# A two-layer convolution/MLP training step: layer-1 pre-activations reloaded half a stage ahead, normalised inputs loaded behind them, and w1-gradient transposes put half a job further on

## The chip, the cores and the metric

The kernel runs on one core of a Trainium2 chip. The metric is the device time of one execution in microseconds. A core has five engines that run their own in-order instruction streams: TensorE (PE in the profile, with its weight loads as PEld), VectorE (DVE), ScalarE (ACT), GpSimd (POOL) and SyncE (SP). SP, POOL and ACT also issue the transfers (DMAs) between the chip's main memory and the on-chip memory.

## The reference

The reference computes a forward pass and all its gradients. With `S = 2048` rows, `D = 448` columns and `F = 1792` hidden columns:

```python
def block_A(x):   # q = layernorm(x); k, v, shift_k, ssm_k, ssm_D are inputs
    kv = shift_conv(k, shift_k) * v              # 4 taps along the sequence
    y  = causal_conv(kv, ssm_k) + kv * ssm_D     # over the whole sequence, by FFT
    return layernorm(x) * y

def block_B(x):
    return silu(layernorm(x) @ w1) @ w2          # 448 -> 1792 -> 448

x = A_q
x = x + block_A(x); x = x + block_B(x)           # "layer 0"
x = x + block_A(x); x = x + block_B(x)           # "layer 1"
out, vjp = jax.vjp(whole, A_q, A_k, A_v, A_shift_k, A_ssm_k, A_ssm_D, w1, w2)
return out, *vjp(grad_out)
```

All inputs and outputs are bf16. `y` depends on no layer's `x`, so it is computed once. The weights are shared by the two layers, so their gradients are sums over the two.

## The kernel before, in words

The program has three parts. The prefix computes `y` by matrix FFTs. The main part does the forward pass of both layers and the backward pass through the MLPs. The suffix computes the gradients of the convolution and of the weights.

In the main part the 2048 rows are cut into four chunks `c` of 512 rows. A stage of the backward pass of layer `L` for chunk `c` is `ga(c, L)` followed by `gn(c, L)`:

- `ga` multiplies the incoming gradient (transposed, `gT`) by `w2T` in seven steps `fp`, each of eight matmuls into `ps_g`. ACT copies each result to `ghp` (line 625; one buffer), and DVE multiplies it by the slope of silu, `dT`, into `ghT` (line 630). After steps 3 and 6 half of `ghT` is turned by DMA transposes and stored to `GH_d` (`store_turned`). These go through SP.
- `gn` multiplies `ghT` by `w1T` for each of four 128-row tiles `tl` into `ps_n` (14 matmuls each). ACT scales the result to `lb_u` (line 668), and a chain of some eleven DVE instructions goes back through the two layernorms (`lb_junk`, `lb_cc`, `G`, `gy`, `gYb`), in layer 0 with one more ACT instruction, `lb_v` (line 646).

For layer 1 the slopes are made from pre-activations that are still on the chip. For layer 0 the forward pass stored the pre-activations to the main memory (`DT_d`, two halves per chunk), because they don't fit; `load_d(c, half)` reads a half back (896 KB, tile `dTl`, three buffers under the tag `D`), and `slope` turns it into silu's derivative in place, with four ACT instructions (line 560). `load_n(c)` reads the normalised inputs `nb_l` and `na_l` (448 KB each).

Which instruction comes first on an engine is decided by a scheduler, from the program's order, the readiness of operands and its own estimates; within an engine or a queue the resulting order is fixed. `tc.issue_after(i)` keeps what stands inside it behind instruction `i` in that order. Before the change, in a stage of layer 0, `slope` of the second half is kept behind the last `lb_u` of the stage before (`k.last_u`), and `slope` of the next chunk's first half stands in the middle of `ga`; that half is loaded at the start of the same stage.

The weight gradients in the suffix are jobs (`_job`): a 512 KB tile `dstat` of stored activations (`A_d`) or gradients (`GH_d`) is loaded through SP, and 16 matmuls multiply it by a 1792 KB operand that stays on the chip: `X` and `GO` (the output's gradient) for w2, `mov3` and `mov1` (normalised inputs) for w1. Two jobs add into one `ps_d`, giving 128 of the 1792 rows of a gradient. The first w2 jobs are fillers: they may be scheduled into gaps of TensorE from a given load on. For w1 the 128 x 448 result has to be stored turned: DVE casts it to `dout`, TensorE transposes it in four pieces into `ps_dt`, ACT copies it to `do`, and POOL stores it:

```python
        o = pool.tile([P, D], BF16, name="dout", tag="dout", bufs=2)
        nc.vector.tensor_copy(o[:], ps[:, :D])
        pt = psum.tile([DC, ND, P], BF16, name="ps_dt", tag="po", bufs=2)
        for dc in range(ND):
            nc.tensor.transpose(pt[:, dc, :], o[:, dc * DC:(dc + 1) * DC], k.ident[:])
```

In the built order these four transposes stand 4 matmuls into the next job pair in most cases, and 5 to 10 in the first four. Beside these jobs DVE computes the gradient of `k` (`gkp`, `gk_acc`, `gk`; lines 982 and 984). `GO` takes the place of `w1` (tag `WA`) and `mov3` that of `w2` (tag `WB`), so neither can be loaded before the forward pass of layer 1 has done with these weights. `mov1` takes the place of `X`.

Of the kernel before, what the change touches and what calls it, by code (L numbers as in the profile page):

```python
# [10 lines left out]
FP32 = mybir.dt.float32  # L11
BF16 = mybir.dt.bfloat16
# [5 lines left out]
P = 128  # L18
S = 2048
D = 448  # L20
F = 1792
J = 16
NT = 16
DC = 112
ND = 4
NF = 14
# [222 lines left out]
def _pm(ap2d):  # L249
    return ap2d.rearrange("(p j) d -> p j d", j=J)  # L250
# [213 lines left out]
class Main:  # L464
# [191 lines left out]
    def gn(self, c, L, ghT, nb, gres, na):  # L656
        nc, k = self.nc, self.k
        sl = slice(4 * c, 4 * c + 4)
        si = 2 * L
        cp = self.ch.tile([P, 8, 2], FP32, name="cp", tag="cp", bufs=1)  # L660
        G = k.X[:, sl, :] if L == 1 else self.ch.tile([P, 4, D], BF16, name="G0", tag="gb", bufs=2)
        for tl in range(4):
            t = 4 * c + tl
            pn = k.psum.tile([P, 512], FP32, name="ps_n", tag="tr" if L == 1 and tl % 2 else "po", bufs=2)
            for ft in range(NF):
                nc.tensor.matmul(pn[:, :D], lhsT=ghT[ft // 7][:, ft % 7, tl * P:(tl + 1) * P], rhs=self.w1T[:, ft, :], start=(ft == 0), stop=(ft == NF - 1))  # L666
            u0 = self.ch.tile([P, D], FP32, name="lb_u0", tag="lb_u0", bufs=2)
            last_u = nc.scalar.activation(u0[:], pn[:, :D], ACT.Identity, scale=k.rstd[2 * L + 1][:, t:t + 1], accum_out=cp[:, tl, 0:1])  # L668
            k.bal.add("act", 0.75)
            k.last_u = last_u  # L670
            g1 = G[:, tl, :]
            self.ln_bwd(u0[:], nb[:, tl, :], cp[:, tl, :], gres(tl), g1)
            if L == 1:
                nc.vector.tensor_tensor(out=k.gYb[:, t, :], in0=g1, in1=na[:, tl, :], op=ALU.mult)
            else:
                gy = self.ch.tile([P, D], BF16, name="gy", tag="lb_junk", bufs=1)
                nc.vector.tensor_tensor(out=gy[:], in0=g1, in1=na[:, tl, :], op=ALU.mult)
                nc.vector.tensor_tensor(out=k.gYb[:, t, :], in0=gy[:], in1=k.gYb[:, t, :], op=ALU.add)
            u1 = self.ch.tile([P, D], BF16, name="lb_u1", tag="lb_u0", bufs=2)
            nc.vector.scalar_tensor_tensor(out=u1[:], in0=g1, scalar=k.rstd[si][:, t:t + 1], in1=self.Y[:, t, :], op0=ALU.mult, op1=ALU.mult, accum_out=cp[:, 4 + tl, 0:1])  # L680
            k.bal.add("dve", 1.2)
            self.ln_bwd(u1[:], na[:, tl, :], cp[:, 4 + tl, :], g1, g1, g1 if L == 0 else None)
        if L == 0:
            nc.gpsimd.dma_start(out=_pm(k.outs[1][0])[:, sl, :], in_=G[:])

    def load_d(self, c, hh):
        nc, k = self.nc, self.k
        t = self.td.tile([P, NF // 2, 512], BF16, name="dTl", tag="D", bufs=3)
        k.d0_load = nc.sync.dma_start(out=t[:], in_=k.DT_d[c, hh])
        return t  # L690

    def load_n(self, c):
# [13 lines left out]
    def run(self):  # L706
        k, nc = self.k, self.nc
        pairs = ((0, 2), (2, 4))
        with self.tc.high_priority():
            self.a_fwd(0, 0, k.x0c0, k.na0, pairs)  # L710
            nT = self.b_tr(self.b_pre(0, 1, pairs, nc.vector))
        cur = []
        self.h(0, 0, nT, 0, cur)
        for c in range(4):
            if c < 3:
                self.a_fwd(c + 1, 0, self.x0_load(c + 1))
                nb = self.b_pre(c + 1, 1)
            else:
                na, nb = self.a_fwd(0, 2, None), self.b_pre(0, 3)
            self.h(c, 0, nT, 1, cur)  # L720
            nT = self.b_tr(nb)
            if c in (1, 2):
                self.load_weights_T(3 - c)
            fol = []
            self.h((c + 1) % 4, 0 if c < 3 else 1, nT, 0, fol)
            self.out(c, cur, False)
            cur = fol
        for c in range(4):
            gb, gT = self.g_pre(c, 1)
            self.h(c, 1, nT, 1, cur)  # L730
            if c < 3:
                na1 = self.a_fwd(c + 1, 2, None)
            self.out(c, cur, True)
            self.turn_plain(c)
            if c == 3:
                d0 = self.load_d(0, 0)
                self.slope(d0)
            box = []
            ghT = self.ga(c, 1, gT, cur, (lambda: box.append(self.b_pre(c + 1, 3))) if c < 3 else None)
            cur = []  # L740
            if c < 3:
                nb1 = box[0]
                nT = self.b_tr(nb1)
                self.h(c + 1, 1, nT, 0, cur)
            else:
                d1 = self.load_d(0, 1)
                nl = self.load_n(0)
                gn = self.g_pre(0, 0)
            self.gn(c, 1, ghT, nb, lambda tl: gb[:, tl, :], na)
            na, nb = na1, nb1  # L750
        for c in range(4):
            with self.tc.issue_after(k.last_u.ins):
                self.slope(d1)
            dT, (nb, na), (gb, gT) = ((None, d0), (None, d1)), nl, gn
            if c == 2:
                k.mov3 = k.wk.tile([P, NT, D], BF16, name="mov3", tag="WB")
                with self.tc.issue_after(k.d0_load.ins):
                    nc.sync.dma_start(out=k.mov3[:], in_=_pm(k.N_d[3][:]))
            if c == 1:
                k.GO = k.wk.tile([P, NT, D], BF16, name="GO", tag="WA")  # L760
                with self.tc.issue_after(k.d0_load.ins):
                    nc.sync.dma_start(out=k.GO[:], in_=_pm(k.grad_out[0]))
            if c < 3:
                d0 = self.load_d(c + 1, 0)
            ghT = self.ga(c, 0, gT, dT, (lambda: self.slope(d0)) if c < 3 else None)
            if c < 3:
                d1 = self.load_d(c + 1, 1)
                nl = self.load_n(c + 1)
                gn = self.g_pre(c + 1, 0)
            self.gn(c, 0, ghT, nb, lambda tl: self.X[:, 4 * c + tl, :], na)  # L770
        self.flush()


def _job(k, ps, src, ft, mov, slot, start, stop):
    pl, tag, bufs = slot
    st = pl.tile([P, NT, P], BF16, name="dstat", tag=tag, bufs=bufs)
    k.nc.sync.dma_start(out=st[:], in_=src[:, ft, :, :])
    for t in range(NT):
        i = k.nc.tensor.matmul(ps[:, :D], lhsT=st[:, t, :], rhs=mov[:, t, :], start=start and t == 0, stop=stop and t == NT - 1)  # L779
    return i  # L780
# [15 lines left out]
def _gw1(k, pool, slots, mov3, mov1):  # L796
    nc, psum = k.nc, k.psum
    out7v = k.outs[7].rearrange("(c p) f -> p c f", p=DC)
    for ft in range(NF):
        ps = psum.tile([P, 512], FP32, name="ps_d", tag="tr", bufs=2)  # L800
        for L, mov in ((1, mov3), (0, mov1)):
            slot = slots.pop(0)
            slots.append(slot)
            _job(k, ps, k.GH_d[L], ft, mov, slot, L == 1, L == 0)
        o = pool.tile([P, D], BF16, name="dout", tag="dout", bufs=2)
        nc.vector.tensor_copy(o[:], ps[:, :D])  # L806
        pt = psum.tile([DC, ND, P], BF16, name="ps_dt", tag="po", bufs=2)
        for dc in range(ND):
            nc.tensor.transpose(pt[:, dc, :], o[:, dc * DC:(dc + 1) * DC], k.ident[:])  # L809
        o7 = pool.tile([DC, ND, P], BF16, name="do7", tag="do7", bufs=2)  # L810
        nc.scalar.copy(o7[:], pt[:])  # L811
        nc.gpsimd.dma_start(out=out7v[:, :, ft * P:(ft + 1) * P], in_=o7[:])  # L812


def _ssm_suffix(k):
    nc, tc, bal = k.nc, k.tc, k.bal
# [3 lines left out]
    psum = k.psum  # L820
    mm = dict(tag="mm", bufs=2)
    k.pt = dict(s1=mm, s2=mm, v=mm)
    with ExitStack() as es:
# [7 lines left out]
        dp2 = pool("dp2")  # L831
        A1 = sp.tile([P, NDH, 2, 16, 4], BF16, name="A1g")
        Z = sp.tile([P, NDH, P], BF16, name="Zg")
        ksf = k.yk.tile([P, J, D], BF16, name="ksf", tag="Y")
        B1k = A1[:].rearrange("p a c n s -> p (a c n s)").rearrange("p (q d) -> p q d", d=D)
        _load_minv(k, nc.gpsimd)
# [2 lines left out]
        with tc.tile_pool(name="sspec2", bufs=1, reuse_waits="tile") as p1:  # L839
# [8 lines left out]
            def spectrum(cp):  # L848
# [3 lines left out]
                t = [kk[:, 0, :], kk[:, 1, :], xsw]  # L852
                nc.gpsimd.dma_start(out=t[0], in_=k.SPEC_d["K"][:, lo:hi])
                nc.gpsimd.dma_start(out=t[1], in_=k.SPEC_d["KV"][:, lo:hi])
                if cp == 2:
                    nc.gpsimd.dma_start(out=ksf[:], in_=_pm(k.KS_d[:]))
                for u in range(2):
# [105 lines left out]
            nc.gpsimd.dma_start(out=o4[0:1536].rearrange("(g b n) -> b g n", g=3, b=4), in_=gsk[:, 0:3, :])  # L963
            nc.gpsimd.dma_start(out=o4[1536:1792].rearrange("(b n) -> b n", b=2), in_=gsk[0:2, 3, :])
        slots = [(k.dp, "dstat", 3)]
        with tc.issue_after(k.d0_load.ins):
            _gw2(k, k.dp, range(4), slots)
        slots = [(k.dp, "dstat", 3), (k.dp, "dstat", 3), (dp2, "dstat", 2), (k.dp, "dstat", 3), (dp2, "dstat", 2)]
        _gw2(k, k.dp, range(4, NF), slots)
# [49 lines left out]
```

## Time and profile before

| what | us |
|---|---|
| median of six runs | 798.3 |
| lowest and highest | 796.33 and 800.05 |
| the profiled execution's own time | 796.33 |
| its span from the first to the last instruction | 794.5 |
| PE busy | 724.7 |
| DVE busy | 516.1 |
| ACT busy | 441.0 |
| POOL busy | 101.7 |

The profile is one execution. Its times are counted from the span's start. Engine rows give the start, the duration, the engine, the line, the operation, the tiles written and read, and in square brackets how long the engine stood idle before and what ended that. A `q` behind an engine's name marks its queue of transfers. The mean granted clock of TensorE was 0.972. In this execution the layer-0 stages of the backward pass lie between about 408 and 551 us, and the w1-gradient jobs from 691 us to the end.

### The profile page before, as it was taken

The page shows a single profiled execution, that of the slowest core. Times are in us where ns is not written, and L with a number is a line of the kernel's source. Part 1 is how long each engine was busy: PE and PEld are TensorE (multiplying, and loading weights), DVE is VectorE, ACT ScalarE, POOL GpSimd, SP SyncE. Part 2 cuts the span into 40 slices and gives each one's busy share as a digit, 9 for nine tenths or more (in the row PEclk, how much of TensorE's full clock was granted, in tenths as well). Part 3 has the DMA queues.
Part 4 walks back from the last instruction along what each step waited for, and adds up shares of the span by engine and source line. Part 5 has one row for each costly group of instructions (what it writes and reads, how often), then busy time and mean ns, then how long its engine had stood idle before and what let it go on. Part 6 is the DMA issues. An engine that isn't in the chain of part 4 may idle for free.

```text
span 794.5 us, 12699 instructions
## 1 busy us (share of the span) xinstructions
PE 724.7 (91%) x4982; PEld 380.5 (48%) x5025; DVE 516.1 (65%) x1056; ACT 441.0 (56%) x551; POOL 101.7 (13%) x168
## 2 busy tenths in 40 slices
PE   6998779999999999999979696999799999989995
PEld 4966534444444434434434332444466765545553
DVE  4789678788435978859467875878456625894100
ACT  4879777766466676876846757545356633000000
POOL 1143212222100010000000000001011123111111
PEclk9999889999999999999999998999999999999999
DMA  9359999998968869889878998989978685777650
GB/s 321 130 171 306 374 219 295 296 278 213 259 169 170 176 183 231 205 176 228 212 226 195 277 295 212 285 209 309 365 211 284 200 307 185 257 237 209 177 177 17
DMA packets 188888, 183.69 MB, mean 231 GB/s; under 512 B 135482, under 2 KB 164030, under 8 KB 187804
## 3 DMA queue, kind: packets, MB, share of 16 engines
q1 hardware_dynamic: 173808, 122.77, 59.3%
q0 software_dynamic: 12688, 52.08, 18.9%
q10 hardware_dynamic: 2332, 8.03, 3.3%
q8 instruction: 39, 0.64, 0.3%
q14 instruction: 21, 0.17, 0.1%
HBM read 76.50 MB, written 65.87 MB: 179 GB/s over the span
## 4 chain that ended last, share of the span: by engine, by line
issue 43%; PE 26%; DVE 14%; ACT 8%; POOL 4%; DMA 3%; POOLq 0%; SPq 0%; ACTq 0%; DVEq 0%
PE ps_o L598 6%; PE ps_d L779 5%; PE ps_h L518 5%; DVE dT L113 3%; DMA kk_c<-spec_KV 2%; PE ps_v L232 2%; DVE ln_st L260 2%; PE ps_v L233 2%; ACT na L274 2%; POOL out_dram L812 1%; PE ps_cv L370 1%; PE ps_gK L911 1%; ACT aT L574 1%; POOL rstd L267 1%; ACT ghp L625 1%
## 5 line engine op out<-in xcount | busy, mean ns | idle before, releaser
L779 PEld LDWEIGHTS <-dstat 128*128 128x128 bf16 x896 | 87.1, 99 | 81.6 <-issue 7.7
L518 PE MATMUL ps_g<-gT,w2T 128*128 128x512 bf16 (+1 forms) x432 | 101.7, 396 | 23.0 <-ACT ghp L625 21.4
L518 PE MATMUL ps_h<-nT,w1sb 128*128 128x512 bf16 (+1 forms) x434 | 102.6, 385 | 6.1 <-DVE dT L113 2.6
L666 PE MATMUL ps_n<-w1T,ghT 128*128 128x448 bf16 x448 | 92.4, 353 | 1.9 <-ACT lb_u L668 1.4
L598 PE MATMUL ps_o<-w2sb,aT 128*128 128x448 bf16 x448 | 90.8, 353 | 0.3 <-ACT aT L574 0.3
L779 PE MATMUL ps_d<-mov,dstat 128*128 128x448 bf16 x448 | 88.9, 357 | 0.6 <-DMA mov<-N_d 0.6
L574 ACT ACTIVATE aT<-ps_h 128x1024 bf16<-128x1024 f32 (+1 forms) x64 | 58.3, 918 | 37.5 <-PE ps_h L518 28.7
L518 PEld LDWEIGHTS <-w2T 128*128 128x128 bf16 (+1 forms) x448 | 37.3, 99 | 85.6 <-issue 56.7
L113 DVE CAST dT<-ps_h 128x1024 bf16<-128x1024 f32 (+1 forms) x56 | 59.3, 1066 | 26.0 <-ACT aT L574 25.9
L625 ACT CAST ghp<-ps_g 128x1024 bf16<-128x1024 f32 x56 | 56.5, 1008 | 34.3 <-DVE ghT L630 18.8
L518 PEld LDWEIGHTS <-w1sb 128*128 128x128 bf16 (+1 forms) x448 | 36.3, 97 | 68.3 <-issue 40.4
L666 PEld LDWEIGHTS <-ghT 128*128 128x128 bf16 x448 | 41.7, 98 | 45.3 <-DVE ghT L630 5.1
L598 PEld LDWEIGHTS <-aT 128*128 128x128 bf16 x448 | 42.1, 98 | 43.0 <-issue 4.3
L811 ACT COPY do<-ps_dt 112x512 bf16<-112x512 bf16 x14 | 8.2, 586 | 87.6 <-PE ps_dt L809 87.6
L232 PE MATMUL ps_v<-Gsb,pa 128*128 128x128 bf16 x336 | 42.7, 221 | 10.2 <-DVE Zg L113 5.0
L779 PE MATMUL ps_d<-X,dstat 128*128 128x448 bf16 x224 | 51.5, 364 | 0.2
L779 PE MATMUL ps_d<-GO,dstat 128*128 128x448 bf16 x224 | 50.5, 356 | 0.2
L806 DVE CAST dout<-ps_d 128x448 bf16<-128x448 f32 x14 | 8.7, 624 | 57.3 <-PE ps_d L779 57.3
L233 PE MATMUL ps_v<-Gsb,pb 128*128 128x128 bf16 x336 | 41.7, 221 | 1.0 <-DVE pb L443 0.7
L668 ACT ACTIVATE lb_u<-ps_n,rstd 128x448 f32<-128x448 f32 x32 | 20.3, 634 | 37.0 <-DVE G L653 16.1
L232 PEld LDWEIGHTS <-pa 128*128 128x128 bf16 x336 | 33.2, 99 | 12.1 <-DVE pa L442 7.0
L630 DVE TENSOR_TENSOR ghT<-dT,ghp 128x1024 bf16<-128x1024 bf16 (+1 forms) x32 | 19.5, 620 | 27.6 <-ACT ghp L625 27.6
(187 smaller groups left out, 1180.9 us busy)
## 6 DMA issues: line engine op xcount, KB each, us to landing
GH_d<-turned SPq DMA_DIRECT2D x16, 896.0 KB, 5.8
dstat<-A_d SPq DMA_DIRECT2D x28, 512.0 KB, 5.1
dstat<-GH_d SPq DMA_DIRECT2D x28, 512.0 KB, 3.8
A_d<-turned SPq DMA_DIRECT2D x12, 896.0 KB, 4.8
DT_d<-dT POOLq DMA_DIRECT2D x8, 896.0 KB, 6.3
dTl<-DT_d SPq DMA_DIRECT2D x8, 896.0 KB, 6.7
spec_K<-Z POOLq DMA_DIRECT2D x7, 512.0 KB, 7.9
KB<-Z POOLq DMA_DIRECT2D x14, 256.0 KB, 12.0
```

The lines of the kernel that those rows point to most:

```text
L113: eng.tensor_copy(out, in_)
L232: nc.tensor.matmul(pv[:, i, :], lhsT=pa[:, i * P:(i + 1) * P], rhs=k.Gsb[:, ga, :], start=True, stop=False)
L233: nc.tensor.matmul(pv[:, i, :], lhsT=pb[:, i * P:(i + 1) * P], rhs=k.Gsb[:, gb, :], start=False, stop=True)
L260: i = nc.vector.bn_stats(out=st[:, tl, :], in_=src(tl))
L518: self.nc.tensor.matmul(ps[:, u, :], lhsT=w[lo:hi, b, f:f + P], rhs=x[lo:hi, b, :], start=(seen[u] == 1), stop=(seen[u] == ND))
L574: last = nc.scalar.activation(a, ps[:, 0:n, :], ACT.Silu)
L598: nc.tensor.matmul(po[:, :D], lhsT=aT[ft // 7][0][:, ft % 7, tl * P:(tl + 1) * P], rhs=self.w2sb[:, ft, :], start=(ft == 0), stop=(ft == N ...
L625: k.last_gh = nc.scalar.copy(gh[:], ps[:])
L630: nc.vector.tensor_tensor(out=ghT[hh][:, o:o + len(u), :], in0=dT[hh][1][:, o:o + len(u), :], in1=gh[:, u[0]:u[0] + len(u), :], op=ALU.mult)
L666: nc.tensor.matmul(pn[:, :D], lhsT=ghT[ft // 7][:, ft % 7, tl * P:(tl + 1) * P], rhs=self.w1T[:, ft, :], start=(ft == 0), stop=(ft == NF - 1))
L668: last_u = nc.scalar.activation(u0[:], pn[:, :D], ACT.Identity, scale=k.rstd[2 * L + 1][:, t:t + 1], accum_out=cp[:, tl, 0:1])
L779: i = k.nc.tensor.matmul(ps[:, :D], lhsT=st[:, t, :], rhs=mov[:, t, :], start=start and t == 0, stop=stop and t == NT - 1)
```

## The change

In layer 0 of the backward pass the first half of the next chunk but one is now loaded behind the second half of the next chunk, at the end of `ga`, so that there are always up to three halves on the chip (`e0` is the third). `slope` of the second half is kept behind the second `lb_u` of the stage before (`k.mid_u`) where it was kept behind the fourth. `load_n` is kept behind the latest `load_d`, where it stood in front of `g_pre`. The load of `GO` goes from stage 1 of layer 0 to the last stage of layer 1, behind the first reload, still on SP. The load of `mov3` goes from stage 2 of layer 0 to the suffix, on POOL; in the built order it stands on POOL ahead of the last store of the output. The filler jobs are kept behind the reload of half (1, 0) where they were kept behind that of (3, 1). In `_gw1` the cast stays where it was, and the transposes, the copy and the store (now `turn`) are kept behind the first job of the next pair, that is, 16 matmuls further on.

```diff
@@ gn
-            k.last_u = last_u
+            if tl == 1:
+                k.mid_u = last_u
@@ load_d
-        k.d0_load = nc.sync.dma_start(out=t[:], in_=k.DT_d[c, hh])
+        k.d_load = nc.sync.dma_start(out=t[:], in_=k.DT_d[c, hh])
@@ run, layer 1
             if c == 3:
                 d0 = self.load_d(0, 0)
                 self.slope(d0)
+                k.GO = k.wk.tile([P, NT, D], BF16, name="GO", tag="WA")
+                with self.tc.issue_after(k.d_load.ins):
+                    nc.sync.dma_start(out=k.GO[:], in_=_pm(k.grad_out[0]))
...
-                d1 = self.load_d(0, 1)
+                d1, e0 = self.load_d(0, 1), self.load_d(1, 0)
+                k.go_jobs = k.d_load
                 nl = self.load_n(0)
                 gn = self.g_pre(0, 0)
@@ run, layer 0
         for c in range(4):
-            with self.tc.issue_after(k.last_u.ins):
+            with self.tc.issue_after(k.mid_u.ins):
                 self.slope(d1)
             dT, (nb, na), (gb, gT) = ((None, d0), (None, d1)), nl, gn
-            if c == 2:
-                k.mov3 = k.wk.tile([P, NT, D], BF16, name="mov3", tag="WB")
-                with self.tc.issue_after(k.d0_load.ins):
-                    nc.sync.dma_start(out=k.mov3[:], in_=_pm(k.N_d[3][:]))
-            if c == 1:
-                k.GO = k.wk.tile([P, NT, D], BF16, name="GO", tag="WA")
-                with self.tc.issue_after(k.d0_load.ins):
-                    nc.sync.dma_start(out=k.GO[:], in_=_pm(k.grad_out[0]))
+            ghT = self.ga(c, 0, gT, dT, (lambda: self.slope(e0)) if c < 3 else None)
             if c < 3:
-                d0 = self.load_d(c + 1, 0)
-            ghT = self.ga(c, 0, gT, dT, (lambda: self.slope(d0)) if c < 3 else None)
-            if c < 3:
-                d1 = self.load_d(c + 1, 1)
-                nl = self.load_n(c + 1)
+                d0, d1 = e0, self.load_d(c + 1, 1)
+                if c < 2:
+                    e0 = self.load_d(c + 2, 0)
                 gn = self.g_pre(c + 1, 0)
             self.gn(c, 0, ghT, nb, lambda tl: self.X[:, 4 * c + tl, :], na)
+            if c < 3:
+                with self.tc.issue_after(k.d_load.ins):
+                    nl = self.load_n(c + 1)
@@ _gw1
+    def turn(ft, o):
         pt = psum.tile([DC, ND, P], BF16, name="ps_dt", tag="po", bufs=2)
         for dc in range(ND):
             nc.tensor.transpose(pt[:, dc, :], o[:, dc * DC:(dc + 1) * DC], k.ident[:])
...
+    hold = None
+    for ft in range(NF):
+        ps = psum.tile([P, 512], FP32, name="ps_d", tag="tr", bufs=2)
+        for L, mov in ((1, mov3), (0, mov1)):
...
+            i = _job(k, ps, k.GH_d[L], ft, mov, slot, L == 1, L == 0)
+            if hold:
+                with k.tc.issue_after(i.ins):
+                    turn(*hold)
+                hold = None
+        o = pool.tile([P, D], BF16, name="dout", tag="dout", bufs=2)
+        nc.vector.tensor_copy(o[:], ps[:, :D])
+        hold = (ft, o)
+    turn(*hold)
@@ _ssm_suffix
+        k.mov3 = k.wk.tile([P, NT, D], BF16, name="mov3", tag="WB")
...
+                if cp == 4:
+                    nc.gpsimd.dma_start(out=k.mov3[:], in_=_pm(k.N_d[3][:]))
...
-        with tc.issue_after(k.d0_load.ins):
+        with tc.issue_after(k.go_jobs.ins):
             _gw2(k, k.dp, range(4), slots)
```

More of the change, by code (lines that the diff above doesn't have):

```diff
@@ L798, in _gw1 @@
     out7v = k.outs[7].rearrange("(c p) f -> p c f", p=DC)
[L799 to L806, printed above, removed]
+    def turn(ft, o):
         pt = psum.tile([DC, ND, P], BF16, name="ps_dt", tag="po", bufs=2)
@@ L812, in _gw1 @@
         nc.gpsimd.dma_start(out=out7v[:, :, ft * P:(ft + 1) * P], in_=o7[:])
+    hold = None
+    for ft in range(NF):
+        ps = psum.tile([P, 512], FP32, name="ps_d", tag="tr", bufs=2)
+        for L, mov in ((1, mov3), (0, mov1)):
+            slot = slots.pop(0)
+            slots.append(slot)
+            i = _job(k, ps, k.GH_d[L], ft, mov, slot, L == 1, L == 0)
[7 more added lines that the diff above has]
+    turn(*hold)
 def _ssm_suffix(k):
```

## The prediction

> **What bounds the kernel now.** I read the page's sections 1 and 2 first, to see which engine carries each part, then the waits of PE, the timeline around them, and last the queues that feed what PE waits for.
>
> ```profile
> PE 724.7 (91%) x4982; PEld 380.5 (48%) x5025; DVE 516.1 (65%) x1056; ACT 441.0 (56%) x551; POOL 101.7 (13%) x168
> ...
> PE   6998779999999999999979696999799999989995
> ```
>
> PE is busy 91% of the span, so what can be gained is its holes. After the prefix the deep ones are slices 21, 23 and 25 (397 to 417, 437 to 457, 477 to 497 us), the layer-0 stages; 29 is the wait for `kk_c`, which the change leaves; 36 (695 to 715) is a shallow one in the w1-gradient stage. The waits of PE from 400 to 535 us name one cause for nearly all of it:
>
> ```profile
> PE ps_g L518 <- ACT ghp L625: 18.8, 10, 6.7
> PE ps_n L666 <- ACT lb_u L668: 1.4, 3, 0.7
> ```
>
> The timeline gives the three long ones, and what ACT did before the late `ghp`:
>
> ```profile
> 414.91 2.19 PE L518 MATMUL ps_g<-gT,w2T 128*128 128x512 bf16 x8 [4.00 <-ACT ghp L625]
> ...
> 456.60 5.23 PE L518 MATMUL ps_g<-gT,w2T 64*128 64x512 bf16 x16 [5.17 <-ACT ghp L625]
> ...
> 490.26 5.46 PE L518 MATMUL ps_g<-gT,w2T 64*128 64x512 bf16 x16 [6.67 <-ACT ghp L625]
> ```
>
> ```profile
> 411.35 1.06 ACT L560 ACTIVATE dTl<-dTl 128x1024 bf16<-128x1024 bf16 x1 [7.34 <-DMA dTl<-DT_d]
> ...
> 450.09 4.40 ACT L560 ACTIVATE dTl<-dTl 128x1024 bf16<-128x1024 bf16 x5
> ...
> 480.58 1.06 ACT L560 ACTIVATE dTl<-dTl 128x1024 bf16<-128x1024 bf16 x1 [2.52 <-DMA dTl<-DT_d]
> ```
>
> The reader is to see that both slope calls of a stage (8 ACT instructions, about 7 us) stand together between the third and the fourth `ghp`, and that two of them also wait for a reload of DT_d. The fourth `ghp` therefore starts at 455.56 and 489.22. PE then also starts cold: 16 matmuls take 5.23 and 5.46 us.
>
> The stage itself is not PE's. The first `lb_junk<-lb_u,nb_l` of a stage on DVE stands at 433.62, 465.01, 498.91 and 527.09, so the stages take 31.4, 33.9 and 28.2 us. DVE has 23 us of work in each and PE 25 to 27, cold clock included. The last of them had no long wait: 28.2 us is the measured floor of this dependency chain (20.2 us of DVE chain up to the fourth `ghT`, then 8.0 us of `ghp`, `ghT` pairs).
>
> The w1-gradient stage ends the program on PE:
>
> ```profile
> PE ps_dt L809 <- DVE dout L806: 3.2, 3, 2.1
> ```
>
> ```profile
> 702.38 0.43 PE L809 MATMUL ps_dt<-ident,dout 128*112 128x128 bf16 x4 [2.14 <-DVE dout L806]
> 702.65 7.33 PE L779 MATMUL ps_d<-mov,dstat 128*128 128x448 bf16 x29
> ...
> 741.74 0.43 PE L809 MATMUL ps_dt<-ident,dout 128*112 128x128 bf16 x4
> 742.00 6.22 PE L779 MATMUL ps_d<-mov,dstat 128*128 128x448 bf16 x32
> ```
>
> One turn waits 2.14 us for its cast, and a steady job takes 6.44 us (741.74 to 748.18) where its matmuls take 6.06 (16 of them 3.03 us, 682.28 to 685.31) and its transposes 0.22.
>
> **The change, part by part.** (a, b) names the reloaded half b of chunk a.
>
> *Slopes.* No work is removed; ACT's 8 instructions per stage stand elsewhere. In the built order of the changed kernel the late half's four come after the second `lb_u` of the stage before, two in front of the first `lb_v` and two behind it, where ACT now idles 1.60 and 1.66 us (waits for `lb_cc` and `G`): they fit to about 0.5 us. The early half's four are spread between the third `lb_u` and the third `ghp`. The queue is in order, so each such piece now holds back what stands behind it until its reload has landed. That is the price to work out.
>
> *Entry into layer 0.* ACT still meets a piece of (1,0) ahead of the third `lb_u`, and (1,0) is still issued behind four transposes (405.43, used at 411.35), so the 4.00 us hole stays. The four pieces of (0,1) at 417.82 to 421.18 us (3.47 us) go, but DVE was busy 4.93 and 4.86 of 5 us from 415 to 425 and would be the next late one: at most 2.5 us come out. Against that, the GO and mov3 loads (1792 KB each, 7.9 and 7.6 us to landing) now fall into 375 to 395 us, ahead of (0,1) and (1,0). DMA there: 243, 304, 218 and 121 GB/s per 5 us, where the best stretches show about 345; part is absorbed, up to 3.6 us of delay is not. Between -1.5 and 2.5; I take 1.0.
>
> *Stage 0 to 1.* Floor 28.2. ACT reaches the first piece of (2,0) at 8.2 us after the stage's start (third `lb_u` 441.05 plus 0.83). Its load stood behind GO: issued 440.15, landed near 449.9. Without GO (0.94 us of issue and about 4 us of sharing) and with `nb_l`, `na_l` behind it I estimate issue at 4.6 and landing at 10.4 (5.8 us, within the 5.4 to 9.8 of this load's eight). Behind the piece stand the first `ghp` and second `lb_v`; DVE wants the `ghT` at 10.7 and gets it at 12.4: 1.7 us. 29.9 against 31.4: 1.4 us gained (0 to 3).
>
> *Stage 1 to 2.* Here `ghp` stands ahead of the piece, so only the second `lb_v` is held, about 0.7 us; (3,0) no longer queues behind mov3. 28.9 against 33.9: 5.0 (3.5 to 6). *Stage 2 to 3:* no early half; 0.4 (0 to 1).
>
> *Loads and queues.* The mov3 load goes from SP to POOL, GO to the end of layer 1. A rule speaks against counting mov3's move as a gain:
>
> ```profile
> 469.93 0.85 SPq L758 DMA_DIRECT2D mov<-N_d  x1
> 470.82 0.43 SPq L689 DMA_DIRECT2D dTl<-DT_d  x1
> ```
>
> The reload behind it landed 9.8 us after its issue (ACT waits until 480.58) where the quickest took 5.4. The Trainium skill ("DMA: Bandwidth & Descriptors", "Issuing engines are not separate DMA queues") says that all issuers share the same 16 engines and another one saves only issue time. By the rule the move of queue is worth the 0.85 us of issue, and the stage 1 to 2 gain would be about 1.2 if the bytes stayed there. By the row it is the bytes ahead that cost 4 us, and the change also moves them 87 us earlier, into a stretch with room: I keep 5.0 and put the rule's share into the entry term. On POOL the mov3 load waits for w2 to be free (last `ps_o`, 382.7) and stands in front of the last `out_dram<-X`, which nobody waits for. `nb_l`, `na_l` go from in front of a transpose to behind the second reload; they land some 15 us before their use. If DMA were full there, 2 us each. Three `dstat` loads (512 KB) go in near 408, where DMA moved 14 GB/s from 415 to 420; without that room 2 us each would fall on the chunk-0 transposes, whose tiles nobody but the w1 stage reads.
>
> *w2-gradient fill.* 55 instead of 44 of these matmuls stand ahead of the first `ps_s`, in layer-0 holes, and 8 fewer behind `ps_r`: 8 x 0.189 = 1.5 us, counted below. In between the fills per gap are almost the same, only the job borders shift; the third `out_dram<-dout` now precedes the first `kk_c` loads on POOL, and its cast precedes the last two A1g copies. 0, with 2 us either way.
>
> *w1 transposes.* They now come 16 matmuls (3.03 us) after their job's end instead of 4 to 10. From `ps_r` (672.3) on: 93 matmuls bring the stage's start from 691.4 to 689.9; mov1 lands 7.6 us after X is free, at 694.7; the first job ends 697.7, its turn is due 699.8, and DVE has the cast ready at 700.7 (its order puts the cast after 700.04's row, 1.7 us earlier than now): 0.9 us of wait instead of 2.14. Later turns wait 0.8 and 0.45 behind the `gk` chain, the rest nothing. The fourth turn ends 721.1; 304 matmuls x 0.1894 = 57.6, nine turns 2.0, last cast and turn 0.9: 781.6 against 787.1. Gain 5.4 (3.5 to 6.4), with the 1.5 in it. Here a rule and a row differ:
>
> ```profile
> 703.00:705.00 2.00, 2.00 (x7) 0.50 0.09 30
> ```
>
> The clock is 0.50 there, after a wait of 2.14 us. The Trainium skill ("TensorE: Matmul & The Clock Gate", "HAM oscillation — how this bites in real kernels") only warns of idle gaps above some 3.4 us. By the rule the old wait cost 2.14 and the gain were 3.7; by the row it cost 1.7 more (29 matmuls in 7.33 less about 0.1 of overlap, against 5.5). I take the row. It cuts both ways: if 0.9 us also chills the clock, 1.7 is lost again.
>
> **The sum.** 1.0 + 1.4 + 5.0 + 0.4 + 0 + 5.4 = 13.2 us. The profiled execution took 796.33 us (span 794.5 and 1.83 around it) and would take 783.1. It is the quickest of the six, 2.0 below the median, so against the median: 798.3 - 13.2 = 785.1. Measurement tells 0.2% (1.6 us) from no change.
>
> **The rivals.** *Casts late.* DVE's `gk` chain holds the early casts longer and the clock drops: w1 gains 1, the rest stays: 789.5. For it: DVE was busy 24.5 of 25 us from 680 to 705. Against: the cast now stands earlier in DVE's order. Chance 0.12.
>
> *Reloads as late as today.* If the early halves land 9.8 us after issue still, stage 0 to 1 takes 33.9 (-2.5), stage 1 to 2 32.9 (+1.0), the entry -1.5; with 0.4 and 5.4: 2.8 gained, 795.5. For it: DMA share near 1.0 in most of 430 to 515. Against: 3.6 MB leave these stages. Chance 0.13.
>
> *Slower: ACT stuck at the early half's slope.* At one place in each of three borders, ahead of `lb_v` and `lb_u`, each us of late landing costs one. The gains are used up at 13.2 / 3 = 4.4 us later than I put it, (2,0) and (3,0) at 14.8 instead of 10.4 after the stage's start. At 6 us: 803.1. For it: GO and mov3 now precede both first reloads, and transposes stall SP behind open transfers (4 to 7 us each). Against: it needs more than the 9.8 us seen with 1792 KB directly ahead. Chance 0.12.
>
> *The slopes do not move.* Excluded by the built order.
>
> **How the numbers follow.** Forecast 0.63 (777 to 792). Slower by over 0.2% (above 799.9): the third rival, 0.12, and 0.01 of the second. Within 0.2%: 0.05, from the second and the edge of the third. Faster: 0.82. The range 777 to 795 leaves out about 0.04 below and 0.16 above.
>
> **What would show it.** Right: the waits of PE for `ghp` fall from 18.8 to under 8 us, with one of about 4 near 415 left; the stages take about 30, 29 and 28 us; ACT waits for `dTl` are at most 2 to 3 us after the entry; the clock stays at 1.0 from 425 to 520; the wait of `ps_dt` for `dout` is below 3 us and steady jobs take 6.28. Wrong: an ACT `dTl` row with over 5 us before it in each stage (third rival), or a clock of 0.50 behind the first turns (first rival), or new holes at `kk_c`.

## The result and the profile after

The changed kernel took 790.5 us (median of 16 runs) against 797.9 for the kernel before; the ratio is 0.9895 with a 95% interval of 0.987 to 0.992. A second set of runs (e5 below) gave 0.9935 (0.990 to 0.997). (The ratios leave out executions in a slower state that most of these kernels fall into now and then, five of these 16 among them, so they are not exactly the quotients of the medians.) The forecast was faster, 785.1 in a range of 777 to 795. The time lies in the range; the gain is 8.4 us (1.05% of 798) in the first set and 5.2 in the second, where the sum said 13.2. The profiled execution took 788.84 us, span 787.1.

Page of the changed kernel, sections 1 and 2:

```profile
PE 718.4 (91%) x4982; PEld 379.6 (48%) x5025; DVE 515.4 (65%) x1056; ACT 440.8 (56%) x551; POOL 102.1 (13%) x169
...
PE   6998779999999999999977898996979999999995
```

PE's busy time fell by 6.3 us with the same 4982 instructions, and its mean granted clock rose from 0.972 to 0.978: less of it ran at the low clock. Of the holes of the layer-0 stages two are nearly filled (slices 23 and 25, 433 to 453 and 472 to 492 us, from 6 tenths to 8). The first is not, it takes slices 21 and 22 now (394 to 433), and slice 28 (531 to 551 us) is a new hole. The waits of PE from 400 to 535 us, and then its timeline:

```profile
PE ps_g L518 <- ACT ghp L625: 13.8, 7, 7.9
```

```profile
417.17 3.26 PE L518 MATMUL ps_g<-gT,w2T 128*128 128x512 bf16 x8 [7.89 <-ACT ghp L625]
...
445.41 1.78 PE L518 MATMUL ps_g<-gT,w2T 128*128 128x512 bf16 x8 [2.18 <-ACT ghp L625]
...
476.95 1.79 PE L518 MATMUL ps_g<-gT,w2T 64*128 64x512 bf16 x8 [2.07 <-ACT ghp L625]
...
539.54 0.93 PE L778 MATMUL ps_d<-X,dstat 128*128 128x448 bf16 x2 [4.37 <-DMA dstat<-A_d]
...
574.74 0.23 PE L232 MATMUL ps_v<-Gsb,pa 128*128 128x128 bf16 x1 [5.16 <-DVE Zg L113]
```

The holes of 5.17 and 6.67 us became 2.18 and 2.07, and PE no longer starts at the low clock behind them (8 matmuls take 1.78 us, where 16 took 5.23). But the one at the entry into layer 0 grew from 4.00 to 7.89, and a wait of 4.37 us for a filler's tile came in behind the last stage. The sign to look for, under 8 us of waits for `ghp`, was missed at 13.8, by the entry alone: without its 7.89 they are 5.9. In the w1-gradient stage the turns now come 16 matmuls, one job, behind the end of their own pair of jobs, where they came 4 to 10 behind it. PE's wait for a cast there, and one steady pair of jobs:

```profile
PE ps_dt L802 <- DVE dout L819: 0.7, 1, 0.7
```

```profile
724.94 0.39 PE L802 MATMUL ps_dt<-ident,dout 128*112 128x128 bf16 x4
...
731.21 0.39 PE L802 MATMUL ps_dt<-ident,dout 128*112 128x128 bf16 x4
```

In this trace only the very last turn still waits for its cast, and a pair of jobs takes 6.27 us where it took 6.44.

Executions differ by 2 to 4 us already in the prefix, so I count from one event that all traces have: a wait of PE of 0.76 or 0.77 us for `ghp`, in the last layer-1 stage (387.49 us before, 385.85 after). From there the four layer-0 stages (first `lb_junk<-lb_u,nb_l`) start at 46.1, 77.5, 111.4 and 139.6 us before, and at 48.1, 77.6, 107.3 and 133.8 after. The span then splits as follows.

| stretch | before | after | gain | predicted |
|---|---|---|---|---|
| entry, to the start of stage 0 | 46.1 | 48.1 | -2.0 | 1.0 |
| stage 0 to 1 | 31.4 | 29.5 | 1.9 | 1.4 |
| stage 1 to 2 | 33.9 | 29.7 | 4.2 | 5.0 |
| stage 2 to 3 | 28.2 | 26.5 | 1.7 | 0.4 |
| stage 3 to the first `ps_v` behind `kk_c` | 47.6 | 55.1 | -7.5 | 0 |
| from there to the first `mov3` matmul | 116.7 | 114.7 | 2.1 | 1.5 |
| from there to the last w1 transposes | 95.7 | 90.1 | 5.6 | 3.9 |
| prefix, up to the event | 387.5 | 385.9 | 1.6 | - |

The prefix is not changed up to a few loads, and its 1.6 us is within what executions of one kernel differ by. The last row ends with the start of the last transpose. Without the prefix the gain is 6.0 us in this pair of traces.

### The profile page after: what moved, and what is told of

It is laid out like the page before. It is cut to its first block, busy times and chain, and to the rows that moved or that the text cites. A ratio compares the mean times of both kernels' runs of the same rounds, so it can differ in the third digit from the quotient of the medians.

```text
span 787.1 us, 12702 instructions
## 1 busy us (share of the span) xinstructions
PE 718.4 (91%) x4982; PEld 379.6 (48%) x5025; DVE 515.4 (65%) x1056; ACT 440.8 (56%) x551; POOL 102.1 (13%) x169
## 4 chain that ended last, share of the span: by engine, by line
PE 30%; DVE 19%; issue 17%; ACT 17%; DMA 11%; POOL 4%; SPq 0%; POOLq 0%; DVEq 0%; ACTq 0%
PE ps_h L518 6%; PE ps_d L778 5%; PE ps_o L598 4%; ACT ghp L625 3%; DMA dTl<-DT_d 3%; PE ps_g L518 3%; DVE dT L113 3%; ACT dT L560 2%; DVE ghT L630 2%; PE ps_n L666 2%; DMA kk_c<-spec_KV 2%; PE ps_v L232 2%; ACT na L274 2%; PE ps_v L233 2%; DVE lb_junk L641 2%
## 5 line engine op out<-in xcount | busy, mean ns | idle before, releaser
L518 PE MATMUL ps_g<-gT,w2T 128*128 128x512 bf16 (+1 forms) x432 | 99.0, 385 | 18.1 <-ACT ghp L625 16.4
L778 PE MATMUL ps_d<-mov,dstat 128*128 128x448 bf16 x448 | 87.2, 352 | 1.0 <-DMA mov<-N_d 1.0
L778 PE MATMUL ps_d<-X,dstat 128*128 128x448 bf16 x224 | 53.6, 369 | 4.5 <-DMA dstat<-A_d 4.4
L778 PE MATMUL ps_d<-GO,dstat 128*128 128x448 bf16 x224 | 49.5, 353 | 0.2
L668 ACT ACTIVATE lb_u<-ps_n,rstd 128x448 f32<-128x448 f32 x32 | 20.3, 633 | 33.1 <-DVE X L653 12.1
```

The lines of the kernel that those rows point to most:

```text
L518: self.nc.tensor.matmul(ps[:, u, :], lhsT=w[lo:hi, b, f:f + P], rhs=x[lo:hi, b, :], start=(seen[u] == 1), stop=(seen[u] == ND))
```

## The experiments

All runs were timed against the kernel before. e1 to e4 share one chip; e5 to e8, and then e9 to e12, were run together on another.

**e1, the w1 transposes alone, and e2, all but them.**

```diff
# e1: before.py with the new _gw1 (turn, hold, issue_after)
# e2: the changed kernel with _gw1 as before
```

> The kernel before with one part of the change: the w1-gradient transposes put 16 matmuls on; reloads, slopes, GO, mov3 and fills as before. Theory A (the two traces: from the first mov3 matmul to the last transpose 95.5 us before, 89.9 after): this part alone is worth 5.6 us, so about 0.993 of the time before; no PE wait for dout but the last, no clock of 0.50 near 703, jobs of 6.28 us. Rival B (the prediction's working): waits of 0.9, 0.8 and 0.45 us remain at the first turns and the part alone is worth 3.9 us (0.995). Rival C (the gain in that stage comes from the earlier start of the stage, not from the turns): under 1 us.

> The changed kernel with the w1-gradient transposes put back where they stood; the reloads, slopes, GO, mov3 and fills as changed. Theory A (7.45 us gained by the last layer-0 stage, of which only ten fill matmuls, 1.9 us, are left at 575 us): 1.9 us faster than before, ratio 0.9976, 5.6 us slower than the changed kernel; PE waits 4 us or more for a dstat tile near 539 us. Rival D (the 7.45 us of the stages do reach the end): 0.991 of the time before.

Measured: e1 0.9952 (0.993 to 0.997), 3.8 us; e2 0.9944 (0.992 to 0.997), 4.5 us. Together 8.3, about the 8.4 of the whole change in its first set. For e1 the prediction's 3.9 was near, and theory A's 5.6 lies at the edge of the interval (2.1 to 5.6). The traces say why: the stretch from the first `mov3` matmul to the last transposes takes 91.9 us in e1 and 93.5 in e2, where the first pair of traces had 90.1 and 95.7. Over all traces of this document it is 89.7 to 92.3 us in the twelve with the turns put on, and 93.5 and 95.7 in the two without. PE's waits, e1 first and then e2:

```profile
PE ps_dt L803 <- DVE dout L820: 2.0, 3, 0.8
```

```profile
PE ps_dt L808 <- DVE dout L805: 2.0, 3, 0.9
```

With the old order (e2) the first turn waited 0.9 us, not 2.14, and the clock stayed at 1.0, so the wait of 2.14 us and the slow 3.4 us behind it in the profile of before do not belong to that order as such. In e2 the stages gain as in the changed kernel (start of stage 3 at 133.6), but the wait for `dstat` is there again (2.83 us). Rival D, that all 7.45 us reach the end, fails; theory A's 1.9 us is below the interval (2.7 to 6.1).

**e3, the load of Minvs put behind the fourth pair of kk_c loads.**

```diff
-        _load_minv(k, nc.gpsimd)
         for n2 in range(16):
...
+                if cp == 3:
+                    with tc.issue_after(kv_load.ins):
+                        _load_minv(k, nc.gpsimd)
```

> The changed kernel with the 1024 KB load of Minvs (POOL's queue, first used at 634 us) put behind the fourth pair of kk_c loads, near 600 us instead of 526. Theory E (the last two DMA transposes of the backward pass crawl beside POOL's M1s and Minvs loads, and the dstat loads of the fillers stand behind them on SP): the second transpose lands 3 us or more earlier than at 533, the wait of PE for dstat at 539.5 falls from 4.37 to under 1.5 us, the clock keeps 1.0 there, and the run is 4 to 6 us faster than the changed kernel (ratio to before about 0.983). Rival F (the transposes are slow for M1s and the store of G, which are done by 529): the wait shrinks by under 1 us and the time stays within 1 us of the changed kernel (0.9895).

Measured 0.9842 (0.980 to 0.988), the size of theory E; but the changed kernel was not timed beside it, and the intervals touch. The wait behind stage 3 shrank to 1.85 us (theory E said under 1.5), and stage 3 to `ps_v` took 49.5 us. What makes the tile late is in SP's queue; the changed kernel from 505 to 545 us:

```profile
516.44 9.56 SPq L484 DMA_TRANSPOSE turned<-ghT  x2
533.05 0.37 SPq L486 DMA_DIRECT2D GH_d<-turned  x1
533.48 2.69 SPq L776 DMA_DIRECT2D dstat<-A_d  x3
```

The three filler tiles stand behind a store that waits for two transposes, and these landed at 528.9 and 533.0, beside POOL's store of G (517.06) and its loads of M1s (517.66) and Minvs (525.89). The wait appears in every other trace that loads Minvs there, e1 with the kernel before's stages included (3.33 us): 2.2 to 4.9 us, 0.5 in e4; only the profile of before has none. In the four traces with Minvs late it is 1.2 to 2.0 us. The stretch from stage 3 to `ps_v` agrees: 49.5 and 49.4 us in the two traces that move Minvs alone (e3, e11), 51.5 to 55.9 in the eight with the new stages that load it early.

**e4, the fourth to sixth filler tile loaded by ACT.**

```diff
-    k.nc.sync.dma_start(out=st[:], in_=src[:, ft, :, :])
+    n = k.n_job = getattr(k, "n_job", -1) + 1
+    (k.nc.scalar if 3 <= n <= 5 else k.nc.sync).dma_start(out=st[:], in_=src[:, ft, :, :])
```

> The changed kernel with the loads of the fourth to sixth w2-gradient tile (512 KB each) issued by ACT instead of SP; the built order also puts some 16 more fill matmuls into the layer-0 stages. Theory E (what held the tile was SP's order, the load stood behind two transposes that landed at 529 and 533): no PE wait for dstat over 1 us between 520 and 560, the kk_c loads issue 4 us or more before 554.8, and the run is 4 to 7 us faster than the changed kernel (ratio to before 0.981 to 0.985). Rival G (the DMA engines themselves are full there, whoever issues): the tiles land as late, the wait stays near 4 us and the time within 1 us of the changed kernel. Rival H: ACT's in-order stream is held by the issues, stages longer, slower than the changed kernel.

Measured 0.9903 (0.987 to 0.994), no better than the changed kernel. The waits of PE from 520 to 620 us:

```profile
PE ps_v L232 <- DVE Zg L113: 11.9, 1, 11.9
PE ps_d L779 <- DMA dstat<-A_d: 0.5, 1, 0.5
```

None of the theories had this. The wait for the tile is nearly gone (0.5 us), so what had held it was its place on SP. But of the `kk_c` loads, issued 3.6 us earlier (551.2), the slowest took 22.5 us to land instead of 20.3, and the next wait took 11.9 us instead of 5.2: in this trace the gain ahead of the gate was lost at it. Why the loads took as long is not shown. It is no rule either: in e3, e7 and e9 that wait stayed at 5.2 to 5.6 us, and their gains went through.

**e5, the changed kernel again, and e6, Minvs and ksf late.**

```diff
# e6: e3, and
-                if cp == 2:
-                    nc.gpsimd.dma_start(out=ksf[:], in_=_pm(k.KS_d[:]))
+                if cp == 4:
+                    with tc.issue_after(kv_load.ins):
+                        nc.gpsimd.dma_start(out=ksf[:], in_=_pm(k.KS_d[:]))
```

> The changed kernel unaltered, as the level for the three beside it, on the same chip. By its earlier runs: 0.9895 of the time before (0.987 to 0.992). If the wait for dstat near 539 us belongs to the change and not to one execution, its trace has it again, between 2.8 us (the trace of the kernel with the transposes put back, the same order up to there) and 4.4 us.

> The changed kernel with Minvs behind the fourth pair of kk_c loads and ksf (1792 KB, first used near 655 us) behind the fifth, where ksf was issued at 547 us, ahead of the first kk_c. Theory I (the next gate after the dstat wait is the landing of the first kk_c loads, 16 to 20 us after their issue behind ksf): the wait of PE for Zg near 571 to 575 us falls from 5.2 to under 2.5 us, and the run is 2 to 4 us faster than with Minvs alone moved (ratio 0.979 to 0.982). Rival J (the kk_c loads wait for the four dstat and two gks tiles, not for ksf): the wait stays near 5 us, ratio 0.984. Rival K: the later loads collide with later kk_c loads, slower than 0.984.

Measured: e5 0.9935 (0.990 to 0.997), with a wait of 4.87 us for `dstat` and, at the entry, one of 10.14 us. e6 0.9943 (0.991 to 0.997), the same. Theory I was half right; PE's waits from 520 to 620 us in e6:

```profile
PE ps_v L233 <- DVE pb L889: 7.6, 2, 5.8
PE ps_d L778 <- DMA dstat<-A_d: 2.0, 1, 2.0
PE ps_v L232 <- DVE Zg L113: 1.1, 1, 1.1
```

The wait for `Zg` fell from 5.2 to 1.1 us as expected, and came back at 615 us as 5.8 for `pb`, behind the later `kk_c` loads (rival K). From `ps_v` to `mov3` e6 takes 122.4 us, the changed kernel 114.7.

**e7, the first slope of half (1,0) behind the fourth lb_u, and e8, the three edits together.**

```diff
+            def mid():
+                if c == 0:
+                    with self.tc.issue_after(k.last_u.ins):
+                        self.slope(e0)
+                else:
+                    self.slope(e0)
-            ghT = self.ga(c, 0, gT, dT, (lambda: self.slope(e0)) if c < 3 else None)
+            ghT = self.ga(c, 0, gT, dT, mid if c < 3 else None)
```

> The changed kernel with one edit: the first slope of half (1,0) kept behind the fourth lb_u of layer 1's last stage, where it stood ahead of the third lb_u. Theory L (at the entry ACT waits 7.6 us for this reload with two lb_u behind it, and PE 7.9 us for ghp): PE's hole near 417 us falls from 7.9 to under 4.5 us and the first lb_junk of stage 0 comes at 430 to 431 instead of 433.9. At the end 3 us of it arrive if nothing else binds (ratio 0.986). Rival M (the later wait for dstat or for kk_c takes the gain): stage 0 starts earlier, the end within 1 us of the changed kernel. Rival N (DVE was the next late one at the entry): the hole falls but the stage starts within 1 us of 433.9.

> The three edits together on the changed kernel: Minvs late, ksf late, first slope of (1,0) behind the fourth lb_u. If the gates are in series, each reaches the end: 3 us from the entry, 4 to 5 from Minvs, 2 to 4 from ksf, so 9 to 12 us faster than the changed kernel, ratio to before 0.975 to 0.978. If the stretch from 520 to 575 us is bound by transfers whatever stands before it, no better than the kernel with Minvs and ksf alone (0.980 to 0.984).

Measured: e7 0.9807 (0.977 to 0.984), e8 0.9783 (0.975 to 0.982). Against e5 on the same chip e7 is 10 us faster by the ratios, where I expected 3 to 4. ACT at the entry, first the changed kernel, then e7 (the fourth `lb_u` and the slope of (1,0)), and e7's waits of PE from 395 to 520 us:

```profile
402.56 3.47 ACT L560 ACTIVATE dTl<-dTl 128x1024 bf16<-128x1024 bf16 x4 [0.20 <-DMA dTl<-DT_d]
...
413.60 1.06 ACT L560 ACTIVATE dTl<-dTl 128x1024 bf16<-128x1024 bf16 x1 [7.57 <-DMA dTl<-DT_d]
414.56 0.62 ACT L668 ACTIVATE lb_u<-ps_n,rstd 128x448 f32<-128x448 f32 x1
```

```profile
415.79 0.64 ACT L668 ACTIVATE lb_u<-ps_n,rstd 128x448 f32<-128x448 f32 x1
416.61 3.47 ACT L560 ACTIVATE dTl<-dTl 128x1024 bf16<-128x1024 bf16 x4
```

```profile
PE ps_g L518 <- ACT ghp L625: 7.7, 7, 2.8
```

In the changed kernel ACT stands idle for 7.57 us before the slope of (1,0), which nothing needs for another stage, with the third `lb_u` and a `ghp` behind it. With that order undone, stage 0 starts 41.9 us after the common event instead of 48.1 (50.9 in e5). Over all traces with these loads it starts at 41.9 to 45.2 us in the five with the slope moved, and at 47.6 to 50.9 in the six without. My size was off because I let the hole fall only to 4.5 us: at the entry no wait of PE for `ghp` in e7 exceeds 1.5 (the 2.8 is a later one). e8 is 12 us faster than e5 by the ratios, the upper end of what I expected, but only 2 us faster than e7, within the intervals; from `ps_v` to `mov3` it takes 121.6 us, about as long as e6. That each of the three gates gives its part at the end is not shown. The kernel before also has the first piece of that slope ahead of the third `lb_u`, and there ACT waited 7.34 us for (1,0) and PE 4.00; this part of the time was to be had without the change too.

**e9, the loads of GO and mov3 back in the layer-0 stages.** Each is kept behind the late half's reload and stands directly ahead of (2,0) and (3,0).

```diff
+                if c == 0:
+                    k.GO = k.wk.tile([P, NT, D], BF16, name="GO", tag="WA")
+                    with self.tc.issue_after(k.d_load.ins):
+                        nc.sync.dma_start(out=k.GO[:], in_=_pm(k.grad_out[0]))
+                if c == 1:
+                    k.mov3 = k.wk.tile([P, NT, D], BF16, name="mov3", tag="WB")
+                    with self.tc.issue_after(k.d_load.ins):
+                        nc.sync.dma_start(out=k.mov3[:], in_=_pm(k.N_d[3][:]))
```

> The changed kernel with the loads of GO and mov3 (1792 KB each) back on SP in the layer-0 stages, directly ahead of the reloads of (2,0) and (3,0). Theory P (they delay the entry: in 374 to 391 us they hold the DMA transposes of the last layer-1 stage, so the reloads (0,1) and (1,0) are issued 4 us later than in the kernel before): (1,0) is issued about 18 us after the first long ps_g wait of that stage instead of 21.5, PE's hole near 417 falls from 7.9 to 4 us, and stage 0 starts 3 to 4 us earlier, at 44 to 45 us after that point instead of 48.1. In exchange (2,0) and (3,0) land 9 to 10 us after their issue instead of 5.4 and 5.9, and the two stages lengthen by 3 to 4 us each (row), or by 1 us each if only the issue counts (the rule about queues). Sum: 3 to 4 us slower than the changed kernel by the row, 2 faster by the rule. Rival Q (the entry is late because two reloads and two slopes now stand there): the hole stays above 7 us.

Measured 0.9792 (0.974 to 0.984): by the ratios 8 to 11 us faster than the changed kernel, where I expected 3 to 4 slower or 2 faster. Theory P is right on the entry and both its prices for the stages are wrong. SP's queue at the entry, first the changed kernel, then e9 (start, time spent issuing; the reloads (0,1) and (1,0) are the `dTl` rows):

```profile
388.37 8.73 SPq L484 DMA_TRANSPOSE turned<-ghT  x2
397.19 1.19 SPq L690 DMA_DIRECT2D dTl<-DT_d  x1
...
400.82 6.44 SPq L484 DMA_TRANSPOSE turned<-ghT  x2
407.36 0.92 SPq L690 DMA_DIRECT2D dTl<-DT_d  x1
```

```profile
389.15 4.80 SPq L484 DMA_TRANSPOSE turned<-ghT  x2
393.99 0.89 SPq L690 DMA_DIRECT2D dTl<-DT_d  x1
...
397.00 7.19 SPq L484 DMA_TRANSPOSE turned<-ghT  x2
404.28 0.84 SPq L690 DMA_DIRECT2D dTl<-DT_d  x1
```

From the common event, (1,0) is issued after 21.5 us in the changed kernel and 17.7 in e9. ACT's order at the entry is the same in both; e9 waits 3.45 us for (1,0) instead of 7.57, PE 3.47 instead of 7.89, and stage 0 starts at 43.3 instead of 48.1. What delays SP is the traffic beside the two transposes: their issue takes 8.5 to 10.0 us in all eleven traces with GO and mov3 loaded there, and 4.8 in the three without (before, e1, e9). On POOL's queue that traffic is the mov3 load; shares of the DMA engines from 384 to 394 us, changed kernel, then e9:

```profile
q0 software_dynamic: 224, 2.29, 54.1%
```

```profile
q0 software_dynamic: 80, 0.46, 11.0%
```

(GO, on SP, had landed by 382.7, but what stood behind it on SP was late too; the two loads were not tried apart.) In the stages (2,0) and (3,0) land 9.3 and 8.9 us after their issue, near the 9.8 and 9.7 of before, and yet the stages take 29.1 and 28.1 us, less than the changed kernel's 29.5 and 29.7. The built order answers that: with 1792 KB ahead of the reload it puts the early half's slope behind the fourth `lb_u`, and ACT waits 0.60 us at most, where the changed kernel meets it ahead of that and waits 1.64 and 2.10. ACT's slope of (2,0), changed kernel, then e9:

```profile
443.40 1.06 ACT L560 ACTIVATE dTl<-dTl 128x1024 bf16<-128x1024 bf16 x1 [1.64 <-DMA dTl<-DT_d]
```

```profile
444.63 2.01 ACT L560 ACTIVATE dTl<-dTl 128x1024 bf16<-128x1024 bf16 x2 [0.60 <-DMA dTl<-DT_d]
```

So e9's stages differ in ACT's order as well as in the loads, and how much each gives was not separated. From the common event to the last transposes e9's trace is 9.8 us ahead of the changed kernel's: 4.8 at the entry, 1.8 in the stages, 3.6 between stage 3 and `ps_v`, -0.4 behind that.

**e10, e7 again; e11, e7 with Minvs late; e12, e7 with the fillers started as before the change.** The edits are those of e7 and e3; e12 keeps the fillers behind half (3,1).

> The kernel with the first slope of (1,0) behind the fourth lb_u once more, as the level for the two that build on it, on the same chip: 0.981 of the time before (0.977 to 0.984 in its first runs).

> That kernel with Minvs loaded behind the fourth pair of kk_c loads and ksf left where it is. Theory E (Minvs holds the last transposes, and these the dstat tile): 3 to 5 us faster than without it, ratio 0.975 to 0.977, the wait for dstat near 534 us below 2 us. Rival F: within 1 us of the kernel without it; the earlier gain was a difference of chips.

> The kernel with the entry mended and the filler jobs started where they were before the change, behind half (3,1). Theory R (the earlier start of the fillers uses up the three tiles on the chip before the last stage and so makes the wait for dstat): no wait for dstat over 1 us, faster by 2 us or more than with the early start. Rival S (the fourth tile stands behind the last two transposes on SP whatever the start; the early start is worth the ten matmuls, 1.9 us, that it puts into holes): the wait stays at 2 to 5 us, and the run is 1 to 3 us slower.

Measured: e10 0.9836 (0.979 to 0.989), e11 0.9795 (0.974 to 0.985), e12 0.990 (0.984 to 0.996). By the ratios e11 is 3.3 us faster than e10, the size of theory E, and its wait for `dstat` is 1.2 us against 3.1; the intervals overlap, so Minvs's share is likely rather than shown. e12 is 5.1 us slower than e10 by the ratios (these intervals overlap too), and its wait is 3.8 us: theory R, which had no such wait, fails, and the sign is rival S's. At its first `ps_v` e12 has 777 filler and w1 matmuls still to do, e10 has 758; the 19 are 3.6 us, and the rest of the difference is within the intervals.

The best are e8, e9 and e11 (medians of 782.4, 783.3 and 782.0, ratios of 0.978 to 0.980), not to be told apart, and all clear of the changed kernel. e9 with the entry mended and Minvs late was not run.

## Why the prediction was right, and where its sum was wrong

*Direction and cause: right; the total by some luck.* The time lies in the range, but the sum was 13.2 us and the gain 8.4 or 5.2. In the table the entry and the stretch behind stage 3 came out 3.0 and 7.5 us worse than said, and most of the other terms somewhat better. PE's waits for `ghp` inside the stages shrank as the two slope calls were pulled apart, and the clock stayed at 1.0 from 422 to 527 us. The stages took 29.5, 29.7 and 26.5 us (30, 29 and 28 predicted). (2,0) landed 5.4 us after its issue, 9.5 after the stage's start (10.4 predicted), (3,0) 5.9. ACT's waits for them were 1.64 and 2.10 us. The "measured floor" of 28.2 us was no floor: with both slopes out of the way stage 2 to 3 took 26.5 (and 28.2 again in e1, which has the old order).

*Entry: the first step that failed.* The text said that GO and mov3 "now fall into 375 to 395 us, ahead of (0,1) and (1,0)" and that "up to 3.6 us of delay is not" absorbed, and then took +1.0. It was the bound that came true: (1,0) was issued 3.6 us later than before, counted from the common event, ACT waited for it with an `lb_u` behind it, and the term was -2.0 (from -1.4 to -4.8 in the other traces with that order). That is the third rival's mechanism at one of its three borders; at the other two the same waits cost ACT only 1.64 and 2.10 us. Without the loads (e9, one trace) the entry gains 2.8, about the 2.5 that I had allowed.

*mov3 and GO: the second.* "I keep 5.0 and put the rule's share into the entry term." Both sides of that choice were wrong. The row was right that bytes ahead make a reload land 9 us after its issue, but e9 shows that the stages need not pay for it. The entry bears out the Trainium skill ("DMA: Bandwidth & Descriptors", "Issuing engines are not separate DMA queues") in that the engines are shared: with mov3 on POOL's queue, and GO just ahead on SP, SP's two transposes took 8.7 us instead of 4.8. Moving both loads, which the prediction counted as a gain, cost 8 to 11 us as a whole by e9, the change in ACT's order that came with it included.

*Between: the third.* "0, with 2 us either way" was -7.5 in the first two traces. e1 and e2, which have the two orders again, give 50.2 and 51.9 us for that stretch, e5 55.9; so it is 48.9 before and 54.3 after on average, -5.4, of which ten matmuls done ahead (1.9) come back later. I named the fillers, the third store and the casts, and not that the filler tiles stand on SP behind the last two transposes, so that a stage that ends 6 us earlier only meets them earlier. e4 shows the place on SP as the cause of that wait; Minvs as what slows the transposes there is likely, and the rest of the 5.4 us stays open.

*w1 stage: right mechanism, and a size that came right by luck.* 3.9 predicted for the turns alone, 3.8 (2.1 to 5.6) measured. But I had taken the row (clock 0.50 after a wait of 2.14 us) over the rule of the Trainium skill ("TensorE: Matmul & The Clock Gate", "HAM oscillation — how this bites in real kernels"), which warns of idle gaps above some 3.4 us. In e12 a wait of 2.24 us at the same place left the clock alone; its turn, then the window behind it (the clock is the third figure from the end):

```profile
701.55 0.43 PE L810 MATMUL ps_dt<-ident,dout 128*112 128x128 bf16 x4 [2.24 <-DVE dout L827]
```

```profile
703.00:705.00 2.00, 2.00 (x12) 1.03 (x11) 1.93 (x4) 0.00 (x0) 1.06 (x2) 1.00 0.49 154
```

So the low clock need not follow a wait of that length. In the fourteen traces, from 400 us on, PE has 30 waits of 1.7 to 2.7 us, and six of them were followed by a clock of 0.50 within 1.2 us; all 37 waits of 2.8 us or more were, seven of them below that rule's 3.4 us. The 1.7 us that I booked for the clock were one execution's chance, and against them stand waits of 0.9, 0.8 and 0.45 us that I left in and that did not come in the changed kernel's trace (in e1 two early turns still wait 1.2 us together).

*Fillers: right sign.* 1.5 us predicted for the earlier start; ten matmuls, 1.9 us, in the first pair of traces, and 19, 3.6 us, between e10 and e12.

## What to carry to other kernels

When a load moves earlier, cost it at the place where it arrives, by the queue that stands there: here two loads taken out of stages that, with ACT's order of e9, could bear them held the transposes, reloads and slopes of the entry. On an in-order engine, put work that nobody needs for another stage behind the work that somebody waits for; undoing that order at the entry was worth about as much as closing the two holes (on average 5.5 us between the two groups of traces, against the 6.1 gained in stages 0 to 2). And before a saving is summed to the end of the program, ask at the next gate (the next tile, the next load) whether it was waiting for the stage at all.

## What the runs showed of the hardware that was not expected

Two DMA transposes of 896 KB in all held SP for 4.8 us in three traces, and for 8.5 to 10.0 in the eleven where another engine's 1792 KB load ran beside them and one on SP just ahead. Waits of PE of 2.14 and 2.24 us at the same instruction were followed by a clock of 0.50 in one execution and 1.00 in another, so a single profile's stretch at the low clock behind a short wait is not a cost to count on; behind waits of 2.8 us or more it came every time. And the same order at the entry started the layer-0 stages between 47.6 and 50.9 us after the common event in six traces, and between 41.9 and 45.2 in five with the slope moved: one trace of each would have put the difference anywhere from 2 to 9 us.
